# The step at which a 32x32 transpose reads its columns, and the engine that rounds w_out

## The chip, the cores and the metric

The kernel runs on one core of a Trainium2 chip. The metric is the time of the program on the device in microseconds (us): the median of several runs, lower is better. A core has five engines that work side by side, each in the fixed order in which its instructions were placed: TensorE (PE: matmuls, with weight loads, PEld), VectorE (DVE), ScalarE (ACT), GpSimd (POOL) and SyncE (SP, which issues DMAs). They wait for one another by semaphores.

## The reference, cut to what matters

```python
def _attn_ref(q, k, v, omega):            # 2 batches, 8 heads, 576 tokens, 64 channels, 128 features
    q_p, k_p = phi(q * scale), phi(k * scale)       # phi: exp of a projection, less its maximum
    kv = einsum('bhsm,bhsd->bhmd', k_p, v)
    z = sum(k_p, axis=2)
    return einsum('bhsm,bhmd->bhsd', q_p, kv) / (einsum('bhsm,bhm->bhs', q_p, z)[..., None] + 1e-06)

def _moe_ref(x, w1, w2, w3, w_out):       # x: 1152 x 512; w3: 1024 x 1024; w_out: 1024 x 512
    h = (x @ w1) * (x @ w2) @ w3
    return h @ w_out

def _moe2_ref(x, domain_probs, w1, w2):   # 4 experts, weighted by normalised domain_probs
    return sum(p[:, e:e+1] * (maximum(x @ w1[e], 0) @ w2[e]) for e in range(4))
```

The result of the attention goes through `_moe_ref`, and that through `_moe2_ref`. The weights w1, w2, w3 and w_out arrive as 64-bit floats.

## The kernel before, in words

Large products are made in three passes: each operand is split into a high part, rounded to the type fp32r, and a low part, the rest, in the same type; high by low, low by high and high by high are added up in PSUM. `split(hi, lo, src)` makes the parts: line 81 copies `src` to `hi` on ScalarE, with rounding, and line 82 subtracts `hi` from `src` on VectorE, or on the engine that is given (`eng`).

`from_f64` loads a 128 x 512 piece of 64-bit numbers as pairs of 32-bit words (tile `f`, of tag `f64`, three buffers) and builds 32-bit floats from them: line 100 scales the high words on ScalarE, line 101 shifts the low words on VectorE (`f64e`), and line 102 joins the two on VectorE. Within a partition, neighbouring high words lie 8 bytes apart. `load_w64` calls `from_f64` and `split`; `load_wo` does so for eight pieces of w_out (`wof`, then `wo`), `load_w12` for w1 and w2 (`w12f`, `w`), both with the subtraction on GpSimd.

`fold(m)` multiplies w3 by w_out ahead of time, in eight blocks (matmuls of line 211). It needs w3 transposed; `fold_transposed(u)` makes the 16 pieces. It loads a piece (`w3f`), and line 194 transposes it on VectorE in 32x32 squares (`w3t`). The columns of one square must be every fourth column of the piece. The kernel before reorders while it builds the floats: through `by_group`, lines 100 and 101 read the words at a step of 32 bytes and write them side by side, so that line 194 reads step by step:

```python
by_group = lambda x: x.rearrange("p (j c g) -> p j g c", j=4, g=4)
r = from_f64([rows[:, :, f:f + P] for f in first], "w3f", by_group)
nc.vector.transpose(t, r)
```

After that `split` makes the parts of `w3T` (line 81 on ScalarE, line 82 on VectorE), which are the weights of line 211.

The program has three stages. In the first (some 0 to 160 us) eight head pairs go through the attention: transposes and products on TensorE, maxima on VectorE (line 301, `mx`), exponentials on ScalarE (line 307, `ek` and `eq`), normalisation on VectorE (lines 378 to 380, `xs`), then transposition (`ps_x`) and a split into `xt`. `place_v` copies v on GpSimd (line 413, `va`). The table `BESIDE` says which loads (`o` for w_out, `w` for w1 and w2), folds (`f`) and gated products (`b`) are placed beside which pair. A scheduler of the framework then sets each engine's order from its own estimate of the instructions' times, so that a change to one instruction can move others on all engines. The second stage is the rest of the gated products, the third the four experts; they do not use `from_f64`, but for the last of w1 and w2.

Of the kernel before, what the change touches and what calls it, by code (L numbers as in the profile page):

```python
# [8 lines left out]
F32 = mybir.dt.float32  # L9
# [3 lines left out]
ACTF = mybir.ActivationFunctionType  # L13
ALU = mybir.AluOpType
AX = mybir.AxisListType

HI, LO = 0, 1
# [28 lines left out]
def attention_moe_kernel(ctx: ExitStack, tc: tile.TileContext, q, k, v, omega, mw1, mw2, mw3, mwo, probs, ew1, ew2, out):  # L46
    nc = tc.nc
# [5 lines left out]
    P = 128  # L53
# [22 lines left out]
    def bank(tag):  # L76
        return ps_p.tile([P, 512], F32, tag=tag, name="ps_" + tag, bufs=BANKS[tag])

    def split(hi, lo, src, eng=None):

        nc.scalar.activation(out=hi, in_=src, func=ACTF.Copy)  # L81
        (eng or nc.vector).tensor_tensor(out=lo, in0=src, in1=hi.bitcast(F32), op=ALU.subtract)  # L82

    def order_like(t, src):
        return t if len(src.shape) == 2 else t.rearrange("p (j g c) -> p j g c", j=src.shape[1], g=src.shape[2])

    def from_f64(srcs, name, order=lambda x: x):


        r = cv.tile([P, 512, 2], U32, tag="f64", name="f64", bufs=3)  # L90
        rows = P // len(srcs)
        for i, src in enumerate(srcs):
            o = r[i * rows:(i + 1) * rows].rearrange("p (k c) w -> p k (c w)", k=src.shape[1])
            nc.sync.dma_start(out=o, in_=src.bitcast(U32))
        low, high = order(r[:, :, 0]), order(r[:, :, 1])
        f = cv.tile([P, 512], F32, tag="f64f", name=name, bufs=2)
        e = cv.tile([P, 512], U32, tag="f64e", name="f64e", bufs=2)
        fb = f.bitcast(U32)

        nc.scalar.activation(out=order_like(f, high), in_=high.bitcast(F32), func=ACTF.Prelu, scale=2.0**-112, alpha=2.0**32)  # L100
        nc.vector.tensor_scalar(out=order_like(e, low), in0=low, scalar1=29, scalar2=None, op0=ALU.logical_shift_right)  # L101
        nc.vector.scalar_tensor_tensor(out=fb, in0=fb, scalar=3, in1=e, op0=ALU.logical_shift_left, op1=ALU.bitwise_or)
        return f

    def load_w64(pool, srcs, name, eng):
        f = from_f64(srcs, name + "f")
        t = pool.tile([P, 2, 512], F32R, tag=pool.name, name=name)
        split(t[:, HI], t[:, LO], f, eng=eng)
        return t


# [26 lines left out]
    w1_p = mctx.enter_context(tc.tile_pool(name="w1", bufs=8, side="right"))  # L138
# [3 lines left out]
    w12, hid, wo, w3o, x2, xf = {}, {}, [], [], {}, {}  # L142

    def load_w12(g):

        for w, src in enumerate((mw1, mw2)):
            src = src[:, g * P:(g + 1) * P].rearrange("(k p) c -> p k c", p=P)
            t = load_w64(w1_p, [src], "w12", nc.gpsimd)
            w12[w, g] = t.rearrange("p a (k c) -> p a k c", k=KD)

    def load_wo():


        hf, g = divmod(len(wo), 4)
        rows = mwo[hf * 512:(hf + 1) * 512].rearrange("(p g) d -> g p d", g=4)[g]
        wo.append(load_w64(w1_p, [rows.unsqueeze(1)], "wo", nc.gpsimd))

    def gated(a_p, bufs, b, g, tags):

        pool = xt_p if len(hid) < XT_BUFS - 2 * KD else h_p  # L160
        ht = hid[b, g] = pool.tile([P, 2, S], F32R, tag=pool.name, name="hid")
        halves = []
        for w in range(2):
            bs = [bank(tags[2 * w + c]) for c in range(2)]
            for kk in range(KD):
                for n, (x, y) in enumerate(PASSES):
                    for c in range(2):
                        nc.tensor.matmul(  # L168
                            out=bs[c][:, :HS], lhsT=w12[w, g][:, x, kk], rhs=xt[b][kk][:, y, c * HS:(c + 1) * HS],
                            start=(kk == 0 and n == 0), stop=(kk == KD - 1 and n == 2),  # L170
                        )
            for c in range(2):
                if w == 0:
                    t = a_p.tile([P, HS], F32, tag="a", name="a", bufs=bufs)
                    nc.scalar.activation(out=t, in_=bs[c][:, :HS], func=ACTF.Copy)
                    halves.append(t)
                else:
                    t, s = halves[c], slice(c * HS, (c + 1) * HS)
                    nc.vector.tensor_tensor(out=t, in0=bs[c][:, :HS], in1=t, op=ALU.mult)  # L179
                    split(ht[:, HI, s], ht[:, LO, s], t)  # L180
# [3 lines left out]
    def fold_transposed(u):  # L184

        m, hf = divmod(u, KF // 4)
        rows = mw3[m * P:(m + 1) * P].rearrange("(j r) f -> r j f", r=SQ)
        first = [hf * 512 + i * P for i in range(4)]  # L190
        by_group = lambda x: x.rearrange("p (j c g) -> p j g c", j=4, g=4)
        r = from_f64([rows[:, :, f:f + P] for f in first], "w3f", by_group)
        t = cv.tile([P, 512], U32, tag="f64e", name="w3t", bufs=2).bitcast(F32)
        nc.vector.transpose(t, r)
        t = t.rearrange("p (j g r) -> p g j r", j=4, g=4)
        wt = cv.tile([P, 2, 512], F32R, tag="w3T", name="w3T", bufs=2)
        hi, lo = (wt[:, x].rearrange("p (g j r) -> p g j r", j=4, g=4) for x in (HI, LO))
        split(hi, lo, t)
        w3T.append(wt)

    def fold(m):

        po = bank(("po", "w")[m % 2])
        n = 0
        for hf in range(KF // 4):
            u = m * (KF // 4) + hf
            while len(w3T) < min(u + 2, KF * (KF // 4)):
                fold_transposed(len(w3T))
            for g in range(4):
                for a, c in PASSES:  # L210
                    nc.tensor.matmul(  # L211
                        out=po, lhsT=w3T[u][:, a, g * P:(g + 1) * P], rhs=wo[hf * 4 + g][:, c],
                        start=(n == 0), stop=(n == 3 * KF - 1),
                    )
                    n += 1
        t = w3_p.tile([P, 2, 512], F32R, tag="w3o", name="w3o", bufs=KF)
        split(t[:, HI], t[:, LO], po)
        w3o.append(t)
# [51 lines left out]
    with ExitStack() as actx:  # L270
# [93 lines left out]
        for b in range(B):  # L364
            t = st.tile([P, H, D1], F32, name=f"vt{b}")
# [164 lines left out]
        for n in range(len(pairs) + 1):  # L530
# [32 lines left out]
            with ExitStack() as order:  # L563

                for ins in (*u.mark, loaded) if u else ():
                    order.enter_context(tc.issue_after(ins))
                for s in BESIDE.get(n, "").split():
                    if s[0] == "w":
                        load_w12(int(s[1]))
                    elif s[0] == "o":  # L570
                        load_wo()
                    elif s[0] == "f":
                        fold(int(s[1]))
                    else:
                        gated(at, 2, int(s[1]), int(s[2]), ("w", "po") * 2)
# [319 lines left out]
```

## Time and profile before

| | |
|---|---|
| median of 3 runs | 669.84 us (669.25 to 671.47) |
| profiled execution: its own time | 670.11 us |
| its span (first to last instruction) | 668.3 us |
| mean granted TensorE clock | 0.996 |
| busy, share of the span | PE 98%, weight loads 94%, DVE 69%, ACT 63%, POOL 18% |

The span is the profiled execution without what lies around it (1.8 us). Busy shares are means over all stages; a busy PE in the profile is one with a matmul in flight, whose end is modelled. A row of a timeline gives the start of a few like instructions, how long they took together, engine, line, tiles, and in brackets how long the engine had been idle just before and what ended that.

### The profile page before, as it was taken

The page shows a single profiled execution, that of the slowest core. Times are in us where ns is not written, and L with a number is a line of the kernel's source. Part 1 is how long each engine was busy: PE and PEld are TensorE (multiplying, and loading weights), DVE is VectorE, ACT ScalarE, POOL GpSimd, SP SyncE. Part 2 cuts the span into 40 slices and gives each one's busy share as a digit, 9 for nine tenths or more (in the row PEclk, how much of TensorE's full clock was granted, in tenths as well). Part 3 has the DMA queues.
Part 4 walks back from the last instruction along what each step waited for, and adds up shares of the span by engine and source line. Part 5 has one row for each costly group of instructions (what it writes and reads, how often), then busy time and mean ns, then how long its engine had stood idle before and what let it go on. Part 6 is the DMA issues. An engine that isn't in the chain of part 4 may idle for free.

```text
span 668.3 us, 12377 instructions
## 1 busy us (share of the span) xinstructions
PE 655.3 (98%) x4831; PEld 628.2 (94%) x4831; DVE 463.4 (69%) x770; ACT 422.0 (63%) x895; POOL 122.8 (18%) x145
## 2 busy tenths in 40 slices
PE   8999999999999999999999999999999999999997
PEld 6788888899999999999899999999999998999997
DVE  3869867776562134357959868868689588687695
ACT  5899648683552234247768768778587777686740
POOL 2321000131240000000022231331331312314200
PEclk9998999999999999999999999999999999999999
DMA  9868433445110002003154484682883855737725
GB/s 253 268 180 206 122 94 95 127 135 182 59 38 1 1 1 64 1 1 94 64 141 129 65 137 99 113 150 40 157 143 32 152 117 90 138 75 105 126 54 174
DMA packets 58090, 70.59 MB, mean 106 GB/s; under 512 B 8816, under 2 KB 43120, under 8 KB 58032
## 3 DMA queue, kind: packets, MB, share of 16 engines
q1 hardware_dynamic: 44704, 49.05, 25.0%
q0 software_dynamic: 12640, 20.19, 20.6%
q8 instruction: 38, 0.62, 0.4%
q10 hardware_dynamic: 688, 0.56, 0.3%
q14 instruction: 20, 0.16, 0.1%
HBM read 47.24 MB, written 22.54 MB: 104 GB/s over the span
## 4 chain that ended last, share of the span: by engine, by line
PE 82%; DVE 4%; issue 4%; ACT 4%; DMA 3%; POOL 1%; SPq 1%; DVEq 0%; ACTq 0%; POOLq 0%
PE ps_f L807 6%; PE ps_f L725 6%; PE ps_po L211 3%; PE ps_x L725 3%; PE ps_w L725 3%; PE ps_et L725 3%; PE ps_et L807 3%; PE ps_t L807 3%; PE ps_kv L807 3%; PE ps_x L807 3%; PE ps_kv L725 3%; PE ps_t L725 3%; PE ps_po L725 3%; PE ps_w L807 3%; PE ps_w L211 3%
## 5 line engine op out<-in xcount | busy, mean ns | idle before, releaser
L759 POOL DMA_DIRECT2D out_dram<-o x98 | 81.6, 901 | 355.5 <-DVE o L784 173.3
L82 DVE TENSOR_TENSOR hs<-hd,hs 128x1024 fp32r<-128x1024 f32 x48 | 58.3, 1218 | 1.6 <-ACT hs L81 1.6
L81 ACT ACTIVATE hs<-hd 128x1024 fp32r<-128x1024 f32 x48 | 50.6, 1056 | 5.7 <-DVE hd L621 4.6
L709 ACT ACTIVATE hd<-hd 128x288 f32<-128x288 f32 x96 | 40.7, 438 | 9.0 <-DVE hd L707 8.7
L725 PE MATMUL ps_f<-x,w1e 128*128 128x288 f32 x288 | 46.2, 294 | 0.0
L621 DVE TENSOR_TENSOR hd<-hd 128x512 f32<-128x512 f32 x64 | 43.9, 686 | 0.8
L621 DVE TENSOR_TENSOR raw<-raw 128x512 f32<-128x512 f32 x64 | 43.9, 686 | 0.5
L807 PE MATMUL ps_f<-w2e,hs 128*128 128x256 f32 x288 | 43.2, 282 | 0.0
L82 DVE TENSOR_TENSOR w2e<-raw,w2e 128x1024 fp32r<-128x1024 f32 x32 | 38.8, 1218 | 5.4 <-ACT w2e L81 5.3
L725 PEld LDWEIGHTS ps_f<-x,w1e 128*128 128x128 f32 x288 | 40.9, 188 | 0.1
L807 PEld LDWEIGHTS ps_f<-w2e,hs 128*128 128x128 f32 x288 | 38.5, 191 | 0.1
L81 ACT ACTIVATE w2e<-raw 128x1024 fp32r<-128x1024 f32 x32 | 33.1, 1054 | 6.3 <-DVE raw L621 3.2
L168 PE MATMUL ps_po<-xt,w 128*128 128x288 f32 x144 | 35.1, 296 | 0.0
L168 PE MATMUL ps_w<-xt,w 128*128 128x288 f32 x144 | 34.9, 297 | 0.0
L82 POOL TENSOR_TENSOR w<-w12f,w 128x512 fp32r<-128x512 f32 x16 | 22.3, 1404 | 65.4 <-ACT w L81 65.4
L82 DVE TENSOR_TENSOR w1e<-raw,w1e 128x1024 fp32r<-128x1024 f32 x24 | 29.3, 1220 | 5.8 <-ACT w1e L81 5.8
L81 ACT ACTIVATE hid<-a 128x288 fp32r<-128x288 f32 x32 | 13.0, 441 | 29.4 <-DVE a L179 29.2
L101 DVE TENSOR_SCALAR f64e<-f 128x512 uint32<-128x512 uint32 x40 | 24.4, 617 | 9.9 <-DMA f<-in_moe_w_dram 7.2
L81 ACT ACTIVATE w1e<-raw 128x1024 fp32r<-128x1024 f32 x24 | 25.4, 1057 | 6.2 <-issue 2.6
L168 PEld LDWEIGHTS ps_po<-xt,w 128*128 128x128 f32 x144 | 25.6, 189 | 0.1
L168 PEld LDWEIGHTS ps_w<-xt,w 128*128 128x128 f32 x144 | 25.3, 188 | 0.0
L781 ACT ACTIVATE o<-ps_f,pr 128x256 f32<-128x256 f32 (+1 forms) x37 | 17.8, 481 | 11.6 <-PE ps_f L807 7.4
(275 smaller groups left out, 1803.6 us busy)
## 6 DMA issues: line engine op xcount, KB each, us to landing
raw<-in_moe_w_dram SPq DMA_DIRECT2D x32, 512.0 KB, 5.4
out_dram<-o POOLq DMA_DIRECT2D x56, 256.0 KB, 5.1
f<-in_moe_w_dram SPq DMA_DIRECT2D x64, 128.0 KB, 3.3
f<-in_moe_w_dram SPq DMA_DIRECT2D x16, 512.0 KB, 4.6
out_dram<-o POOLq DMA_DIRECT2D x42, 128.0 KB, 4.5
f<-in_moe_w_out_dram SPq DMA_DIRECT2D x8, 512.0 KB, 6.5
kr<-in_k_dram SPq DMA_DIRECT2D x8, 256.0 KB, 5.0
vr<-in_v_dram SPq DMA_DIRECT2D x8, 256.0 KB, 5.1
```

The costliest lines, as they stand in the source:

```text
L81: nc.scalar.activation(out=hi, in_=src, func=ACTF.Copy)
L82: (eng or nc.vector).tensor_tensor(out=lo, in0=src, in1=hi.bitcast(F32), op=ALU.subtract)
L101: nc.vector.tensor_scalar(out=order_like(e, low), in0=low, scalar1=29, scalar2=None, op0=ALU.logical_shift_right)
L168: nc.tensor.matmul(out=bs[c][:, :HS], lhsT=w12[w, g][:, x, kk], rhs=xt[b][kk][:, y, c * HS:(c + 1) * HS], start=(kk == 0 and n == 0), stop ...
L211: nc.tensor.matmul(out=po, lhsT=w3T[u][:, a, g * P:(g + 1) * P], rhs=wo[hf * 4 + g][:, c], start=(n == 0), stop=(n == 3 * KF - 1),)
L621: nc.vector.tensor_tensor(out=o, in0=x, in1=y, op=op)
L709: nc.scalar.activation(out=h, in_=src, func=ACTF.Relu)
L725: nc.tensor.matmul(out=ps, lhsT=w1t[a][:, x, kk, g * P:(g + 1) * P], rhs=x2[b, kk][:, y, s], start=(k in "125" and kk == 0 and n == 0), st ...
L759: dma = nc.gpsimd.dma_start(out=out[toks, d], in_=src[rows], **({} if fresh else dict(accum_op=ALU.add))).ins
L781: nc.scalar.activation(out=o, in_=ps, func=ACTF.Copy, scale=pr[:, t, e:e + 1])
L807: nc.tensor.matmul(out=ps, lhsT=t[a][:, x, g, j * P:(j + 1) * P], rhs=w2t[b][:, y, g], start=(k in "15" and g == 0 and n == 0), stop=(k in ...
```

## The change

`from_f64` loses its reordering: all pieces, those of w3 too, are now built in the order in which they are loaded, at a step of 8 bytes. The reordering moves to the input of the transpose, which now reads its columns at a step of four 32-bit numbers, 16 bytes. Apart from that, `split` can round the high part on another engine, and `load_wo` asks for GpSimd: both instructions of that split are now on GpSimd.

```diff
-    def split(hi, lo, src, eng=None):
+    def split(hi, lo, src, eng=None, high=None):
-        nc.scalar.activation(out=hi, in_=src, func=ACTF.Copy)
+        if high is None:
+            nc.scalar.activation(out=hi, in_=src, func=ACTF.Copy)
+        else:
+            high.tensor_copy(out=hi, in_=src)
         (eng or nc.vector).tensor_tensor(out=lo, in0=src, in1=hi.bitcast(F32), op=ALU.subtract)
...
-        low, high = order(r[:, :, 0]), order(r[:, :, 1])
+        low, high = r[:, :, 0], r[:, :, 1]
...
-        nc.scalar.activation(out=order_like(f, high), in_=high.bitcast(F32), func=ACTF.Prelu, scale=2.0**-112, alpha=2.0**32)
-        nc.vector.tensor_scalar(out=order_like(e, low), in0=low, scalar1=29, scalar2=None, op0=ALU.logical_shift_right)
+        nc.scalar.activation(out=f, in_=high.bitcast(F32), func=ACTF.Prelu, scale=2.0**-112, alpha=2.0**32)
+        nc.vector.tensor_scalar(out=e, in0=low, scalar1=29, scalar2=None, op0=ALU.logical_shift_right)
...
-        wo.append(load_w64(w1_p, [rows.unsqueeze(1)], "wo", nc.gpsimd))
+        wo.append(load_w64(w1_p, [rows.unsqueeze(1)], "wo", nc.gpsimd, nc.gpsimd))
...
-        by_group = lambda x: x.rearrange("p (j c g) -> p j g c", j=4, g=4)
-        r = from_f64([rows[:, :, f:f + P] for f in first], "w3f", by_group)
+        r = from_f64([rows[:, :, f:f + P] for f in first], "w3f")
...
-        nc.vector.transpose(t, r)
+        nc.vector.transpose(t, r.rearrange("p (j c g) -> p j g c", j=4, g=4))
```

The scheduler's order moves with it. Line numbers of the attention are one lower in the kernel after (line 307 becomes 306), and lines 81 and 82 become 82 and 85, with the new copy on 84.

The first place is ScalarE between the tail's exponentials and those of the third head pair (`kva`, `ek`, `eq`), where the first three pieces of w_out are made. Before:

```order
L447 ACTIVATE kva<-ps_kv 128x130
L81 ACTIVATE wo<-wof 128x512
L307 ACTIVATE ek<-ps_f,mx 128x128 x4
L81 ACTIVATE wo<-wof 128x512
L307 ACTIVATE ek<-ps_f,mx 128x128 x4
L100 ACTIVATE wof<-f_267 128x512
L81 ACTIVATE wo<-wof 128x512
L307 ACTIVATE eq<-ps_f,mx 128x128 x4
```

The same place after:

```order
L446 ACTIVATE kva<-ps_kv 128x130
L306 ACTIVATE ek<-ps_f,mx 128x128 x8
L100 ACTIVATE wof<-f_267 128x512
L306 ACTIVATE eq<-ps_f,mx 128x128 x4
L446 ACTIVATE kva<-ps_kv 128x130
```

The three copies `wo` have left ScalarE. On GpSimd they stand as copies of line 84; the first two stand ahead of the first two subtractions.

The second place is ScalarE where w3 begins, beside the fourth head pair. Before:

```order
L100 ACTIVATE wof<-f_584 128x512
L454 ACTIVATE eT<-ps_et 128x512
L81 ACTIVATE xt_76<-ps_x 128x512
L100 ACTIVATE w3f<-f_595 128x512
L307 ACTIVATE eq<-ps_f,mx 128x128 x4
L284 ACTIVATE qT<-ps_t 128x512
L81 ACTIVATE wo<-wof 128x512
L307 ACTIVATE eq<-ps_f,mx 128x128 x4
```

After:

```order
L453 ACTIVATE eT<-ps_et 128x512
L82 ACTIVATE xt_76<-ps_x 128x512
L306 ACTIVATE eq<-ps_f,mx 128x128 x4
L283 ACTIVATE qT<-ps_t 128x512
L100 ACTIVATE wof<-f_584 128x512
L306 ACTIVATE eq<-ps_f,mx 128x128 x4
L100 ACTIVATE w3f<-f_595 128x512
```

The last `wof` and the first `w3f` now stand behind the first `eq`.

The third place is VectorE at the same moment. Before:

```order
L101 TENSOR_SCALAR f64e<-f_595 128x512
L301 TENSOR_REDUCE mx<-ps_f 128x4
L102 SCALAR_TENSOR_TENSOR wof<-wof,f64e 128x512
L301 TENSOR_REDUCE mx<-ps_f 128x4
L82 TENSOR_TENSOR xt_76<-ps_x,xt_76 128x512
L102 SCALAR_TENSOR_TENSOR w3f<-w3f,f64e 128x512
L194 STREAM_TRANSPOSE w3t<-w3f 128x512
```

After:

```order
L101 TENSOR_SCALAR f64e<-f_595 128x512
L300 TENSOR_REDUCE mx<-ps_f 128x4
L85 TENSOR_TENSOR xt_76<-ps_x,xt_76 128x512
L300 TENSOR_REDUCE mx<-ps_f 128x4
L102 SCALAR_TENSOR_TENSOR wof<-wof,f64e 128x512
```

The split of `xt_76` now stands ahead of the second maximum and of line 102. From the first fold on (58.8 us of the trace before) the order on PE, DVE and ACT differs at many places: the matmuls of line 211 stand between other pieces of the attention than before.

## Rows read from the trace of the kernel before

**Rows 1.** Page: granted clock of TensorE in 40 slices of 16.7 us, in tenths.

```profile
PEclk9998999999999999999999999999999999999999
```

**Rows 2.** Windows: stretch, its length, busy time by engine, clock, DMA.

```profile
20.00:60.00 40.00, 37.06 (x240) 32.14 (x239) 31.87 (x63) 36.91 (x102) 12.53 (x11) 0.96 0.76 207
60.00:100.00 40.00, 40.00 (x222) 33.66 (x221) 32.52 (x67) 23.41 (x45) 0.62 (x1) 1.00 0.47 126
100.00:160.00 60.00, 59.02 (x451) 53.79 (x451) 44.49 (x89) 40.78 (x95) 11.89 (x9) 1.00 0.45 135
```

**Rows 3.** Timeline of TensorE, its waits between 20 and 60 us.

```profile
26.06 0.60 PE L116 MATMUL ps_x<-ident,xs 128*128 128x128 f32 x4
27.39 1.13 PE L295 MATMUL ps_f<-om,qT 128*128 128x256 f32 x4 [0.73 <-ACT eq L307]
...
29.56 1.13 PE L295 MATMUL ps_f<-om,qT 128*128 128x256 f32 x4 [0.60 <-ACT eq L307]
...
33.98 0.84 PE L116 MATMUL ps_et<-ident,eq 128*128 128x128 f32 x3 [0.59 <-ACT eq L307]
...
50.47 0.33 PE L116 MATMUL ps_et<-ident,eq 128*128 128x128 f32 x1 [0.66 <-ACT eq L307]
51.16 1.08 PE L461 MATMUL ps_x<-kva,eT 128*128 128x65 f32 x8 [0.36 <-DVE xt L82]
...
52.29 1.85 PE L295 MATMUL ps_f<-om,kT 128*128 128x256 f32 x4
```

**Rows 4.** Timeline of ScalarE ahead of those waits.

```profile
22.48 0.63 ACT L81 ACTIVATE wo<-wof 128x512 fp32r<-128x512 f32 x1 [0.52 <-DVE wof L102]
23.14 1.14 ACT L307 ACTIVATE ek<-ps_f,mx 128x128 f32<-128x128 f32 x4
...
26.20 1.14 ACT L307 ACTIVATE eq<-ps_f,mx 128x128 f32<-128x128 f32 x4
...
28.32 1.19 ACT L307 ACTIVATE eq<-ps_f,mx 128x128 f32<-128x128 f32 x4
...
32.99 0.68 ACT L513 ACTIVATE eTt<-ps_et 128x512 f32<-128x512 f32 x1
...
48.99 1.17 ACT L100 ACTIVATE w3f<-f 128x512 f32<-128x512 f32 x1
50.02 1.17 ACT L307 ACTIVATE eq<-ps_f,mx 128x128 f32<-128x128 f32 x4
```

**Rows 5.** Timeline of VectorE at the same places.

```profile
18.96 0.68 DVE L102 SCALAR_TENSOR_TENSOR wof<-wof,f64e 128x512 uint32<-128x512 uint32 x1
19.76 0.43 DVE L101 TENSOR_SCALAR f64e<-f 128x512 uint32<-128x512 uint32 x1
...
20.70 1.75 DVE L102 SCALAR_TENSOR_TENSOR wof<-wof,f64e 128x512 uint32<-128x512 uint32 x1
22.37 0.68 DVE L301 TENSOR_REDUCE mx<-ps_f 128x4 f32<-128x512 f32 x1
...
48.51 0.70 DVE L301 TENSOR_REDUCE mx<-ps_f 128x4 f32<-128x512 f32 x1
...
50.31 0.70 DVE L82 TENSOR_TENSOR xt<-ps_x,xt 128x512 fp32r<-128x512 f32 x1
```

**Rows 6.** Timeline of GpSimd beside the long line 102 of rows 5.

```profile
17.80 0.61 POOL L413 COPY va<-vr 128x512 f32<-128x512 f32 x1 [7.01 <-PE ps_kv L445]
20.63 1.27 POOL L82 TENSOR_TENSOR wo<-wof,wo 128x512 fp32r<-128x512 f32 x1 [2.22 <-ACT wo L81]
```

**Rows 7.** Groups of ScalarE: line 100 at steps of 32 and 8 bytes.

```profile
L100 ACT ACTIVATE w3f<-f 128x512 f32<-128x512 f32 x16 | 19.0, 1197 | 0.8 <-DVE d L379 0.6 <-ACT xt L81 0.2
L100 ACT ACTIVATE w12f<-f 128x512 f32<-128x512 f32 x16 | 10.8, 681 | 6.4 <-POOL w L82 6.4
```

**Rows 8.** Groups of VectorE between 48 and 127 us, the pieces of w3.

```profile
L194 DVE STREAM_TRANSPOSE w3t<-w3f 128x512 f32<-128x512 f32 x16 | 11.3, 706 | 0.2
L101 DVE TENSOR_SCALAR f64e<-f 128x512 uint32<-128x512 uint32 x17 | 10.8, 634 | 1.0 <-DMA f<-in_moe_w_dram 0.9
```

More of the change, by code (lines that the diff above doesn't have):

```diff
@@ L77, in bank, with from_f64 @@
         return ps_p.tile([P, 512], F32, tag=tag, name="ps_" + tag, bufs=BANKS[tag])
-    def split(hi, lo, src, eng=None):
-        nc.scalar.activation(out=hi, in_=src, func=ACTF.Copy)
+    def split(hi, lo, src, eng=None, high=None):
[3 more added lines that the diff above has]
+            high.tensor_copy(out=hi, in_=src)
         (eng or nc.vector).tensor_tensor(out=lo, in0=src, in1=hi.bitcast(F32), op=ALU.subtract)
-    def order_like(t, src):
-        return t if len(src.shape) == 2 else t.rearrange("p (j g c) -> p j g c", j=src.shape[1], g=src.shape[2])
-    def from_f64(srcs, name, order=lambda x: x):
+    def from_f64(srcs, name):
         r = cv.tile([P, 512, 2], U32, tag="f64", name="f64", bufs=3)
@@ L98, in from_f64, with load_w64 @@
         fb = f.bitcast(U32)
-        nc.scalar.activation(out=order_like(f, high), in_=high.bitcast(F32), func=ACTF.Prelu, scale=2.0**-112, alpha=2.0**32)
-        nc.vector.tensor_scalar(out=order_like(e, low), in0=low, scalar1=29, scalar2=None, op0=ALU.logical_shift_right)
+        nc.scalar.activation(out=f, in_=high.bitcast(F32), func=ACTF.Prelu, scale=2.0**-112, alpha=2.0**32)
+        nc.vector.tensor_scalar(out=e, in0=low, scalar1=29, scalar2=None, op0=ALU.logical_shift_right)
         nc.vector.scalar_tensor_tensor(out=fb, in0=fb, scalar=3, in1=e, op0=ALU.logical_shift_left, op1=ALU.bitwise_or)
         return f
-    def load_w64(pool, srcs, name, eng):
+    def load_w64(pool, srcs, name, eng, high=None):
         f = from_f64(srcs, name + "f")
         t = pool.tile([P, 2, 512], F32R, tag=pool.name, name=name)
-        split(t[:, HI], t[:, LO], f, eng=eng)
+        split(t[:, HI], t[:, LO], f, eng=eng, high=high)
         return t
```

## The prediction, made before the kernel ran

> **What bounds the kernel now.** I read the granted clock by slices first, then the busy time of windows, then the timelines of the engines where TensorE stood still. The clock is full but for a dip in the fourth slice and the edges [rows 1]. TensorE is what the time consists of: it is busy for all of 60 to 100 us and for 59.02 of the next 60 us, while VectorE has 22.99 us and ScalarE 35.81 us idle in those 100 us [rows 2]. So the folds, in which all 16 pieces of w3 are made, hide nearly all the work of the other two engines, and what the change saves there can at most win the 0.98 us that TensorE lacks. The stretch that matters is 20 to 60 us: TensorE is busy for 37.06 of 40 us there, and ScalarE, with 36.91, as much [rows 2]. The missing 2.94 us are five waits: 0.73, 0.60, 0.59, 0.66 and 0.36, four of them for `eq` on ScalarE and the last for the split of `xt` on VectorE [rows 3]. I call them A, B, C, D and E. The exponentials are late because pieces of w_out, and at the end of w3, stand among them. Nothing of the change touches the experts, and I carry their time over unchanged.
>
> **The change part by part.**
>
> *Eight copies leave ScalarE.* Each took 0.63 us there [rows 4], some 5 us in all, before 54 us. What that is worth has to be followed wait by wait, for a copy that stood in an idle moment gives nothing.
>
> Wait A. The exponential that ends it runs at 26.20 [rows 4] and follows a chain that slipped at 20.70: line 102 took 1.75 us instead of 0.68 [rows 5], beside GpSimd's first subtraction of 1.27 us [rows 6]. The maximum at 22.37 stood behind it, and so did the copy at 22.48 and `ek` at 23.14 [rows 4, 5]. After the change the first floats are ready at 19.64, the end of the first line 102 [rows 5], and GpSimd then copies, and may not subtract before it has copied the second piece too. If the copy takes what `va` takes, 0.61 us for as many numbers [rows 6], it is over at some 20.3, before line 102 begins at 20.70. That one then takes 0.68 and the maximum comes about 1.0 us earlier; no copy stands before `ek`, and VectorE takes the next maximum ahead of line 102 of the third piece. So `eq` comes about 1.0 us earlier, at 25.2, and TensorE, which has its transposes at 26.06 [rows 3], finds it under way. I take all of A. A wait's bracket begins at a modelled end: four transposes are counted as 0.60 us, and would be followed sooner, so I add 0.15 and take 0.9.
>
> Wait B. The `eq` at 28.32 stands behind the copy of `xt`, which needs those same transposes. They hardly move, so I take 0.2 us of 0.60. Wait C: `eq` at 33.48, behind `eTt` at 32.99 [rows 4], which itself waits for a transposition just finished on TensorE. Two copies disappear ahead of it, and nothing comes of it: I take 0.
>
> Waits D and E. Before `eq` at 50.02 stands the first `w3f` with 1.17 us [rows 4]; its maximum was done at 49.21 [rows 5]. After the change `w3f` stands behind it, and `eq` can begin at about 49.2, 0.8 us sooner. The split of `xt` at 50.31 [rows 5] stood behind one maximum and a line 102, and now comes right after the first maximum, at about 49.3, a whole 1.0 us sooner. Of 0.66 and 0.36, with the same 0.15 on each, 1.3 us in all, some 0.2 remain, since TensorE now makes three transposes there at once. I take 1.1.
>
> *Line 100 of w3 at 8 bytes.* 1197 ns become 681 [rows 7]: 16 times 0.52 is 8.3 us less on ScalarE. The one that counts is moved anyway (D). The others lie under TensorE's matmuls. In 100 to 160 us I take 0.2 of the 0.98 us.
>
> *Line 101 of w3 at 8 bytes.* 634 ns on average [rows 8] become 0.43 us, as for w_out [rows 5]: 16 times 0.2 is 3.3 us less on VectorE, hidden by the 22.99 us. Without that cover they would count whole.
>
> *The transpose at 16 bytes.* The trace shows none. Nearest below is itself at consecutive numbers, 706 ns [rows 8]. Nearest above is line 100, whose step of 32 bytes costs 0.52 us more than 8 [rows 7], so 1.2 us. Which row is nearer? Line 101 is on the same engine and reads at 32 bytes in 634 ns [rows 8], under the 706 ns in which the transpose now moves as many numbers. VectorE thus fetches a number from so far apart at the rate at which the transpose needs them. I take 0.71 and no cost, and keep 1.2 for a rival.
>
> [...]
>
> *The copy on GpSimd.* Between 0.61 us (`va`, no rounding) and 1.27 (the subtraction, which rounds but reads two inputs) [rows 6]; I take 0.61, since one input is read. At 1.27 the first copy ends at 20.9 and meets line 102 for 0.2 us, and A shrinks to about 0.5. GpSimd is busy 12.53 of 40 us [rows 2], so its five more us fit. The first fold starts some us after the last subtraction of w_out ends, so it waits for it in neither case.
>
> *Order.* From the first fold on all orders differ. The work is the same; whether new waits appear is the open term. Before, such an order lost 0.98 us between 60 and 160 us, and I take the same.
>
> Sum: 0.9 + 0.2 + 0 + 1.1 + 0.2 = 2.4 us. From the profiled 670.11 that gives 667.7. This execution lay 0.27 over the median, so in medians 669.84 - 2.4 = 667.4 us.
>
> **The rivals.**
>
> *The dip goes too.* [...] It begins right behind D and E, when TensorE had stood still. [...] For it: the order of the two. Against: A to C caused no dip.
>
> *New waits eat it.* The first `w3f` now stands behind two groups of exponentials and the last `wof`, so the first transposed piece comes 2 to 3 us later (twice 1.17 less what overlaps [rows 4], and a line 100), while TensorE is to reach the first fold earlier. If it stands still for 2 us in the folds that had no idle time before, 669.4, no change.
>
> *Slower: the transpose pays for its step.* If it takes 1.2 us, VectorE has 8.3 - 3.3 = 5.0 us more between 50 and 125 us. Its mean reserve hides that only if it lies where it is needed; each fold waits for its own piece, one transpose after the other. If all 5.0 reach TensorE the time is 667.4 + 5.0 = 672.4. It decides from about 0.9 us a transpose: 16 times 0.2 is then what line 101 gives back, and beyond it VectorE loses.
>
> **How the numbers follow.** Forecast 0.43, with a range of its own of 666.7 to 668.7 (below: most of the rest of B and C won too; above: A halved and 0.9 us of new waits). Dip gone 0.20; new waits 0.25, from 668.4 to 671; slower 0.12. A change of 0.3%, 2.0 us, is about the least that a measurement tells from none here: faster is below 667.8. That takes 0.31 of the forecast, all of the dip's 0.20 and a little of the rest: 0.53. Within it: 0.12 of the forecast and most of the new waits, 0.34. Slower 0.13, the transpose and a very bad order. The range of 665.4 to 670.8 leaves out a dip gone with more gains, and the slower cases.
>
> **What would show it.** Right: `w3f` at about 0.68 and line 101 at 0.43 us; `w3t` near 0.71; copies of line 84 near 0.61; line 102 beside them at 0.68 and not 1.75; TensorE's idle time in 20 to 60 us at 1.2 us or less, with only B and C left; idle time of 60 to 160 us about 1 us. Wrong: `w3t` over 0.9; idle time or waits for `w3T` inside the folds; waits D and E still there because the maximum or the transposes came later than I think; or the first fold standing still for its piece.

## The result: slower by half a per cent

Six runs of the kernel after have a median of 674.3 us (672.4 to 675.35), six of the kernel before beside them 671.26. The ratio is 1.0052, with a 95% interval of 1.0029 to 1.0074: slower, and outside the range of the prediction. (All ratios here are estimated from all runs taken side by side, and can differ by some 0.1% from the quotient of two medians, which is 1.0045 here.) The profiled execution of after took 673.34 us, with a span of 671.5 us, 3.2 us more than before.

I read the profile after in the order of the prediction. The granted clock by slices answers to [rows 1]:

```profile
PEclk9999999899999999999999999999999999999999
```

There is again one dip, but it stands in the eighth slice, not the fourth. By the mean clocks of the windows (0.96 over 40 us before, 0.97 over 60 us after) I estimate that it costs about as much as the old one, 4% of 40 us and 3% of 60 us, so these two profiles do not differ by it. The windows answer to [rows 2], the first 20 us added:

```profile
0.00:20.00 20.00, 16.45 (x94) 12.34 (x95) 8.46 (x17) 10.82 (x31) 4.87 (x18) 1.00 0.96 266
20.00:60.00 40.00, 38.05 (x262) 33.62 (x261) 31.21 (x62) 32.56 (x95) 17.44 (x19) 1.00 0.70 201
60.00:100.00 40.00, 39.43 (x221) 32.22 (x221) 35.40 (x71) 21.73 (x55) 0.62 (x1) 1.00 0.54 136
100.00:160.00 60.00, 56.45 (x409) 50.57 (x408) 41.35 (x81) 35.73 (x86) 11.35 (x9) 0.97 0.39 115
```

From 20 to 60 us TensorE lacks 1.95 us instead of 2.94: the gain is there. From 60 to 160 us it lacks 0.57 + 3.55 = 4.12 us instead of 0.98: this loss is three times the gain. (In the first 20 us it lacks 3.55 us where before lacked 2.53. This stretch varies among profiles whatever the order: 16.66 to 17.47 us busy in five kernels with the copy on ScalarE, 16.45 to 18.71 in three with the order of after. Of the 3.2 us between these two profiles 1.0 lies here; but kernel one below, which loses as much, is busier here than before, with 18.71 us, so I do not count it to the change.)

TensorE's timeline between 28 and 51 us answers to [rows 3]:

```profile
29.44 1.13 PE L294 MATMUL ps_f<-om,qT 128*128 128x256 f32 x4 [0.53 <-ACT eq L306]
31.23 0.33 PE L116 MATMUL ps_et<-ident,eq 128*128 128x128 f32 x1 [0.66 <-ACT eq L306]
...
34.19 0.85 PE L116 MATMUL ps_et<-ident,eq 128*128 128x128 f32 x3 [0.51 <-ACT eq L306]
...
47.67 0.66 PE L116 MATMUL ps_t<-ident,qr 128*128 128x128 f32 x4 [0.26 <-DVE kT L281]
...
50.16 0.84 PE L116 MATMUL ps_et<-ident,eq 128*128 128x128 f32 x3
50.84 1.00 PE L460 MATMUL ps_x<-kva,eT 128*128 128x65 f32 x8
```

Waits A, D and E are gone, as predicted. B and C are still there, and two have come, 0.66 us behind B and 0.26 for `kT`. At the other end of the first stage TensorE's timeline shows what was not foreseen:

```profile
121.73 1.17 PE L210 MATMUL ps_w<-wo,w3T 128*128 128x512 f32 x4
...
123.88 1.16 PE L318 MATMUL ps_f<-omh,kT 64*128 64x128 f32 x16 [0.19 <-ACT eq L331]
125.97 0.66 PE L116 MATMUL ps_et<-ident,eq 128*128 128x128 f32 x4 [0.93 <-ACT eT L453]
127.19 1.11 PE L460 MATMUL ps_x<-kva,eT 128*128 128x65 f32 x8 [0.57 <-DVE xt L85]
129.59 4.62 PE L210 MATMUL ps_w<-wo,w3T 128*128 128x512 f32 x12 [1.29 <-DVE w3T L85]
```

Four waits in 6 us, 2.98 us together, and then a fold whose twelve matmuls take 4.62 us at a mean clock of 0.63, where twelve at a clock of 1.00 took 3.04 (at 80.72 us of the same trace): the dip. The chain of work through this place, each row the start, the length, the engine, the tile and the line:

```profile
121.65 0.62 ACT eq L331 x2
...
122.41 1.41 ACT eq L331 x5
123.83 0.56 ACT w3f L100
...
124.41 0.70 DVE w3f L102
...
125.14 1.09 DVE w3t L193
126.23 0.31 DVE f64e L101
126.54 0.60 DVE xt L85
127.14 1.20 DVE mx L329 x2
...
128.85 0.69 DVE w3T L85
...
129.59 4.62 PE ps_w L210 x12
```

This is the last piece of w3, made and split for the last fold: line 100 behind eight exponentials, the transpose with 1.09 us, then the split, which stands behind `xt` and two maxima on VectorE. Line 100 of that piece is not later than before, where it also began at 123.7 us, and the transpose even began earlier, at 125.14 against 125.73 us. But the split comes 1.0 us later, at 128.85 instead of 127.87 us. VectorE's split of this piece before:

```profile
127.87 0.68 DVE L82 TENSOR_TENSOR w3T<-w3t,w3T 128x512 fp32r<-128x512 f32 x1
```

What TensorE had to do meanwhile differs too. Its timeline before, at the same time:

```profile
124.48 1.00 PE L445 MATMUL ps_kv<-va,ek 128*128 128x65 f32 x8
...
126.75 1.16 PE L319 MATMUL ps_f<-omh,kT 64*128 64x128 f32 x16
127.84 0.66 PE L116 MATMUL ps_et<-ident,eq 128*128 128x128 f32 x4
128.34 0.60 PE L116 MATMUL ps_x<-ident,xs 128*128 128x128 f32 x4
128.69 2.56 PE L211 MATMUL ps_w<-wo,w3T 128*128 128x512 f32 x10
```

Before, TensorE came to its attention work ahead of this fold at 124.48 us and went through 4 us of it without a wait: the sums of line 445 stood first, and their inputs were there. After, it comes to it at 122.74 us. Some 4 us of attention work stand there too, but most of it waits for fresh results of ScalarE and VectorE, and the sums of line 444 follow behind the fold (at 135.63 us).

The durations, as groups by line of the whole execution, and line 101 between 48 and 127 us (answering to [rows 7] and [rows 8]):

```profile
L193 DVE STREAM_TRANSPOSE w3t<-w3f 128x512 f32<-128x512 f32 x16 | 17.6, 1099 | 0.2
L100 ACT ACTIVATE w3f<-f 128x512 f32<-128x512 f32 x16 | 10.9, 689 | 8.7 <-DVE w3t L193 5.8 <-DVE d L377 2.3 <-DMA f<-in_moe_w_dram 0.6
L84 POOL CAST wo<-wof 128x512 fp32r<-128x512 f32 x8 | 5.4, 687 | 15.4 <-DVE wof L102 11.5 <-DVE d L377 3.9
L102 DVE SCALAR_TENSOR_TENSOR wof<-wof,f64e 128x512 uint32<-128x512 uint32 x8 | 5.4, 683 | 1.1 <-ACT wof L100 1.1
L101 DVE TENSOR_SCALAR f64e<-f 128x512 uint32<-128x512 uint32 x17 | 7.2, 422 | 1.0 <-DMA f<-in_moe_w_dram 1.0
```

The transpose takes 1099 ns and not 0.71 us. The others came about as predicted (the copy with 0.69 us for 0.61). So two suspects are left, the order and the transpose, with line 100's gain against them.

### The profile page after: what moved, and what is told of

Same layout as the page of the kernel before. It is cut to its first block, busy times and chain, and to the rows that moved or that the text cites. A ratio compares the mean times of both kernels' runs of the same rounds, so it can differ in the third digit from the quotient of the medians.

```text
span 671.5 us, 12381 instructions
## 1 busy us (share of the span) xinstructions
PE 655.5 (98%) x4831; PEld 627.6 (93%) x4831; DVE 463.3 (69%) x770; ACT 410.3 (61%) x887; POOL 127.4 (19%) x153
## 4 chain that ended last, share of the span: by engine, by line
PE 85%; DVE 6%; ACT 3%; DMA 3%; issue 2%; SPq 1%; POOL 0%; DVEq 0%; ACTq 0%
PE ps_f L806 6%; PE ps_f L724 6%; PE ps_x L724 3%; PE ps_w L724 3%; PE ps_et L724 3%; PE ps_et L806 3%; PE ps_kv L806 3%; PE ps_t L806 3%; PE ps_x L806 3%; PE ps_w L168 3%; PE ps_kv L724 3%; PE ps_f L168 3%; PE ps_po L168 3%; PE ps_t L724 3%; PE ps_po L724 3%; PE ps_w L806 3%
## 5 line engine op out<-in xcount | busy, mean ns | idle before, releaser
L210 PE MATMUL ps_w<-wo,w3T 128*128 128x512 f32 x96 | 26.0, 421 | 1.3 <-DVE w3T L85 1.3
L101 DVE TENSOR_SCALAR f64e<-f 128x512 uint32<-128x512 uint32 x40 | 22.2, 563 | 6.6 <-DMA f<-in_moe_w_dram 3.4
```

What stands on the lines that cost most here:

```text
L101: nc.vector.tensor_scalar(out=e, in0=low, scalar1=29, scalar2=None, op0=ALU.logical_shift_right)
L210: nc.tensor.matmul(out=po, lhsT=w3T[u][:, a, g * P:(g + 1) * P], rhs=wo[hf * 4 + g][:, c], start=(n == 0), stop=(n == 3 * KF - 1),)
```

## The experiments

My theory: the order that the scheduler made once the copy had left ScalarE costs more than the copy gives; the transpose adds a little, and line 100 at 8 bytes gives some of it back. The rival: the transpose's 16 × 0.39 = 6.3 us is the loss, and the waits of the new order are its consequence.

The built orders allow a clean separation. Before, after, and the first four kernels below have only two orders of instructions between them: with the copy on ScalarE that of before, with the copy on GpSimd that of after. How lines 100, 101 and 194 step through a piece moves no instruction.

**One: the copy alone.** The kernel before with the diff of `split`, `load_w64` and `load_wo` and nothing else.

```diff
-        wo.append(load_w64(w1_p, [rows.unsqueeze(1)], "wo", nc.gpsimd))
+        wo.append(load_w64(w1_p, [rows.unsqueeze(1)], "wo", nc.gpsimd, nc.gpsimd))
```

> The kernel before with the second part of the change alone: the high parts of w_out are rounded by GpSimd, w3 is built and transposed as before. Theory P (the price of the transpose's step made the change slow, and the part for w_out is what I took it for): the transpose stays at 706 ns, TensorE's idle time in 20 to 60 us falls from 2.94 to some 2 us, and the ratio to the kernel before is 0.996 to 0.999. Theory O (the order that the scheduler makes of it, with GpSimd's copies in VectorE's way, made it slow): 1.003 or more, with new waits after 60 us.

Measured: 674.43 us, ratio 1.0065 (1.0043 to 1.0087). Its window from 100 us, and two rows of TensorE's timeline in it:

```profile
100.00:160.00 60.00, 57.42 (x408) 51.53 (x406) 39.01 (x80) 37.93 (x86) 11.58 (x9) 0.94 0.38 115
```

```profile
126.51 1.11 PE L119 MATMUL ps_et<-ident,eq 128*128 128x128 f32 x4 [1.39 <-ACT eT L457]
...
129.76 4.69 PE L214 MATMUL ps_w<-wo,w3T 128*128 128x512 f32 x12 [0.43 <-DVE w3T L85]
```

The loss is all there with the transpose untouched, and TensorE waits at the same place, ahead of the same fold. In this profile the idle time is smaller than in after (2.58 us against 3.55), and the dip behind it is longer (clock 0.94 over the 60 us). `eT` is later than in after, because line 100 of `w3f` stands ahead of it with 1.2 us. The rival falls as the whole cause.

**Two: the steps alone.** The kernel after with the copy back on ScalarE.

```diff
-        wo.append(load_w64(w1_p, [rows.unsqueeze(1)], "wo", nc.gpsimd, nc.gpsimd))
+        wo.append(load_w64(w1_p, [rows.unsqueeze(1)], "wo", nc.gpsimd))
```

> The change without its second part: w3 is read at 8 bytes and transposed at 16, the high parts of w_out stay on ScalarE. P: the transpose takes about 1.1 us as in the kernel after, and the ratio to the kernel before is 1.005 to 1.010, at least that of the whole change. O, with GpSimd to blame: 0.998 to 1.002.

Measured: 669.93 us, ratio 0.9985 (0.9964 to 1.0005), with transposes of 1096 ns. The windows from 60 to 160 us:

```profile
60.00:100.00 40.00, 40.00 (x222) 33.69 (x222) 34.74 (x69) 20.50 (x48) 0.79 (x2) 1.00 0.47 126
100.00:160.00 60.00, 59.63 (x453) 54.57 (x452) 45.15 (x88) 38.19 (x94) 12.04 (x10) 1.00 0.43 131
```

TensorE lacks 0.37 us here, less than before (0.98), though each transpose takes 0.39 us more.

**Three and four: the steps taken apart.** The third is after with the transpose reading number by number (line 100 still at 8 bytes), the fourth is before with the transpose at 16 bytes (line 100 still at 32). The third leaves the regrouping of w3's columns out and the fourth does it twice, so columns of w3 meet other rows of w_out; the work is the same in kind and amount.

```diff
-        nc.vector.transpose(t, r.rearrange("p (j c g) -> p j g c", j=4, g=4))
+        nc.vector.transpose(t, r)
```

```diff
-        nc.vector.transpose(t, r)
+        nc.vector.transpose(t, r.rearrange("p (j c g) -> p j g c", j=4, g=4))
```

> The kernel after, but the transpose reads its squares from neighbouring numbers, so that the columns of w3 are paired with the wrong rows of w_out: its time is read, not its numbers. Every engine has the same instructions in the same order as in the kernel after; only the step of 16 transposes differs. P: the transpose is back at about 0.71 us, the waits of TensorE at 80 us and from 123 to 134 us are gone or below 1.5 us in all, and the ratio to the kernel before is 0.992 to 0.997. O: the waits stay, 1.003 to 1.006.

> The kernel before, but its transpose reads at a step of 16 bytes what was already reordered, so that the columns of w3 are paired with the wrong rows of w_out: its time is read, not its numbers. Every engine has the same instructions in the same order as in the kernel before. P: the transpose takes about 1.1 us, VectorE has 6.3 us more in the folds, TensorE waits for w3T there, and the ratio to the kernel before is 1.004 to 1.010. O: the step is hidden, 0.999 to 1.002.

Measured: the third 672.21 us, ratio 1.0025 (1.0006 to 1.0044); the fourth 672.44 us, ratio 1.0026 (1.0005 to 1.0046), its transposes 1093 ns. Both miss the ranges of both theories and lie nearer to O: the step is not all hidden, but it is not the loss. The six kernels together, with the mean time of those runs whose mean granted clock was 0.997, and the number of runs in which it was 0.999 or 1.000:

| copy and order | line 100 of w3 | transpose reads | kernel | ratio | at clock 0.997 (runs) | at 0.999 or 1.000 |
|---|---|---|---|---|---|---|
| ScalarE, of before | 32 bytes | side by side | before | 1 | 670.68 us (13) | 9 of 34 |
| ScalarE, of before | 32 bytes | 16 bytes | four | 1.0026 | 672.56 us (8) | 4 of 12 |
| ScalarE, of before | 8 bytes | 16 bytes | two | 0.9985 | 670.54 us (3) | 6 of 12 |
| GpSimd, of after | 32 bytes | side by side | one | 1.0065 | 674.30 us (6) | 0 of 11 |
| GpSimd, of after | 8 bytes | side by side | three | 1.0025 | 672.53 us (5) | 4 of 12 |
| GpSimd, of after | 8 bytes | 16 bytes | after | 1.0052 | 673.88 us (5) | 0 of 6 |

(The runs of before counted here are the 34 beside one to four; after was run at another time.)

Each edit is priced twice, by differences of the ratios. The transpose: +0.26% (four less before) and +0.27% (after less three), 1.8 us. Line 100 at 8 bytes: -0.41% (two less four) and -0.40% (three less one), 2.7 us. The copy with its order: +0.65% (one less before) and +0.67% (after less two), 4.4 us. The sum, 0.26 - 0.41 + 0.65 = +0.50%, meets the measured +0.52%, but that is the same comparison once more, since the three edits lead from before to after. One difference by itself is uncertain by some 0.2 to 0.3%, as the intervals show; that the pairs agree makes it firmer. That they agree to 0.02% is luck: by quotients of medians the pairs are +0.33 and +0.16, -0.37 and -0.33, +0.63 and +0.50%. I price line 101's step with line 100's, since the same edit moved both.

One rival remains: that the kernels differ by the dip of the clock alone. The last two columns settle most of it. One and after have no run at 0.999 or 1.000, so part of their loss is the clock. But at the same clock of 0.997, as far as three to 13 runs tell, the copy with its order still costs 3.6 us (one less before) and 3.3 (after less two), the transpose 1.9 and 1.4, and line 100 still gives 2.0 and 1.8.

The third kernel's window, and its fold in TensorE's timeline:

```profile
100.00:160.00 60.00, 56.83 (x422) 51.21 (x421) 40.52 (x83) 36.62 (x88) 11.39 (x9) 1.00 0.41 121
```

```profile
129.82 3.06 PE L210 MATMUL ps_w<-wo,w3T 128*128 128x512 f32 x12 [1.29 <-DVE w3T L85]
```

It has no dip (clock 1.00) although TensorE lacks 3.17 us, and the same fold waits 1.29 us for `w3T` as in after; so the dip is not the loss, but comes on top of it in some runs.

**Five: another order from about 122 us on.** If the cause is the order at the last fold, another order there must take the loss back. The table of the work beside each pair now puts the load of the first parts of w1 and w2 (`w0`) ahead of the last fold, and the scheduler places the rest anew:

```diff
-BESIDE = {..., 5: 'f5 f6', 6: 'f7 w0', 7: 'w1 b00 w2', 8: 'b01 w3'}
+BESIDE = {..., 5: 'f5 f6', 6: 'w0 f7', 7: 'w1 b00 w2', 8: 'b01 w3'}
```

> The kernel after with one entry of the table swapped: beside the seventh pair the first load of w1 and w2 stands before the last fold, not behind it. GpSimd's copies, all steps, and the order up to about 115 us stay. Theory W (the waits of TensorE from 123 to 134 us, for eT, for xt and for the last w3T, are the price of the new order): these waits fall from 3.6 us to below 1.5, the clock does not fall behind them, and the ratio to the kernel before is 0.997 to 1.001. Rival G (GpSimd's copies cost by what they hold up before 60 us, or the whole order is worse): 1.004 to 1.006, as in the kernel after.

Measured: 671.25 us, ratio 1.0006 (0.9988 to 1.0025). The order on the engines that compute differs from after's only from about 122 us on. Its window, and TensorE's timeline:

```profile
100.00:160.00 60.00, 58.66 (x427) 53.41 (x425) 41.06 (x83) 35.22 (x84) 11.38 (x9) 0.97 0.42 128
```

```profile
125.24 0.66 PE L116 MATMUL ps_et<-ident,eq 128*128 128x128 f32 x4 [0.93 <-ACT eT L453]
...
127.10 3.11 PE L168 MATMUL ps_po<-xt,w 128*128 128x288 f32 x12
...
132.88 3.00 PE L210 MATMUL ps_w<-wo,w3T 128*128 128x512 f32 x12
```

Matmuls of a gated product (line 168, which uses w1 and w2) now fill the time in which the last piece is made, the fold no longer waits for it, and 0.46% of the loss comes back with the copy still on GpSimd and the transposes still at 16 bytes. That the dip would go too was expected and did not happen in this profile: it now slows line 168 (3.11 us for twelve that take 1.75 in after). Whether the same swap would win as much in the order of before was not run; but TensorE lacks only 0.98 us there from 100 to 160 us, at full clock [rows 2], so there is less to win.

**Six: another priority.** The attention of a pair has a priority of its own, set by `offset`: -100 for the first six pairs and 400 from the seventh on. Here 400 begins with the sixth.

```diff
-            with tc.high_priority(offset=-100 if n < 6 else 400):
+            with tc.high_priority(offset=-100 if n < 5 else 400):
```

> The kernel after with the attention's raised priority from the sixth pair on instead of the seventh; GpSimd's copies and all steps stay, and the order differs from about 80 us on. W: another order without last pieces of w3 among the attention's copies on ScalarE; TensorE's idle time of 60 to 160 us is about 1 to 2 us instead of 4.1, and the ratio to the kernel before 0.998 to 1.002. G: 1.004 to 1.006.

Measured: 669.81 us, ratio 0.9988 (0.9971 to 1.0006). The order differs from after's from about 48 us on VectorE and 68 us on TensorE, and not from 80 us as I expected. Its profile (671.53 us, above its own median) still lacks 3.26 us from 100 to 160 us, at other places; the idle time that I expected was wrong, the ratio was not. A second order thus takes back what the first lost, but its profile does not show where. Part of it is the clock: seven of its 12 runs have a mean clock of 0.999 or 1.000, none of after's six, and the profiled one has 0.997.

**Seven to ten: no step at all.** If w_out's rows are loaded in another order, w3 needs no regrouping: line 100 at 8 bytes and the transpose number by number, and each column of w3 still meets its row of w_out. The seventh loads each piece in one transfer with one more dimension in its source, the eighth is that with the GpSimd copy and the table of experiment five; the ninth uses four transfers a piece, the tenth is that with the GpSimd copy and the priority of experiment six. Of the two source forms the lines that choose the rows are shown.

```diff
-        rows = mwo[hf * 512:(hf + 1) * 512].rearrange("(p g) d -> g p d", g=4)[g]
+        rows = mwo[hf * 512:(hf + 1) * 512].rearrange("(i g c) d -> g i c d", i=4, g=4)[g]
...
-        nc.vector.transpose(t, r.rearrange("p (j c g) -> p j g c", j=4, g=4))
+        nc.vector.transpose(t, r)
```

```diff
-        rows = mwo[hf * 512:(hf + 1) * 512].rearrange("(p g) d -> g p d", g=4)[g]
+        at = [hf * 512 + i * P + g * SQ for i in range(4)]
+        rows = [mwo[a:a + SQ].unsqueeze(1) for a in at]
...
-        nc.vector.transpose(t, r.rearrange("p (j c g) -> p j g c", j=4, g=4))
+        nc.vector.transpose(t, r)
```

> No reordering anywhere: the rows of w_out are loaded so that the columns of a 32x32 square of w3 may be neighbours; line 100 and line 101 read w3 at 8 bytes, the transpose reads number by number, and the high parts of w_out stay on ScalarE. The order on every compute engine is that of the kernel before. Theory S (in a fixed order the steps add up: 16-byte transposes cost 0.26% and line 100 at 8 bytes wins 0.4%, as the four runs so far give): 0.9985 - 0.0027 = 0.996 to the kernel before. Rival H (the gains are of the order of what the runs scatter, and hidden where TensorE has other work): 0.998 to 1.000.

> The run before this one without reordering, the rows of w_out loaded to fit, so that the transpose reads number by number: the same instructions in the same order on every compute engine. W and S together: 0.27% below the run before this one, 0.994 to 0.998 to the kernel before. G: 1.001 to 1.003.

> As the run with no reordering and the high parts on ScalarE, but each piece of w_out comes in four loads of 32 partitions, as those of w3 do, instead of one load with a split outer dimension. The order on every compute engine is that of the kernel before. S: the late loads of w_out are gone, the transpose takes 0.71 us, line 100 of w3 0.68, and the ratio to the kernel before is 0.995 to 0.998. H: 0.998 to 1.000. If small loads are what was slow there, and not the split dimension: above 1.02 again.

> The run with the attention's priority raised from the sixth pair on, without reordering: four loads for a piece of w_out, and the transpose reads number by number; on every compute engine the order of that run. W and S together: 0.27% below that run's 0.9988, that is 0.994 to 0.998 to the kernel before. G or H: 0.998 to 1.001.

Measured: 696.48 us (1.0382, 1.0354 to 1.0410), 697.35 (1.0391, 1.0358 to 1.0424), 674.49 (1.0061, 1.0037 to 1.0086) and 673.89 (1.0069, 1.0042 to 1.0095). All are slower, and in all of them TensorE lacks more from 20 to 60 us than before, while loads are late. Of the seventh, the loads of v by queue, kind, count, size and median us from issue to landing, and its window:

```profile
vr<-in_v_dram SPq DMA_DIRECT2D x8, 256.0 KB, 14.9
```

```profile
20.00:60.00 40.00, 28.19 (x141) 24.09 (x142) 16.40 (x32) 22.71 (x64) 7.52 (x7) 0.74 0.44 144
```

With the one transfer a piece, v, which comes through the same queue, takes 14.9 us (16.5 in the eighth), 5.2 in after, and TensorE lacks 11.8 us there. How long the transfer itself takes, and why v is late behind it, the trace does not show. With four transfers v lands after 4.2 us, but a piece of w_out comes late. The ninth's window and its first wait:

```profile
20.00:60.00 40.00, 36.21 (x205) 30.88 (x204) 25.36 (x56) 31.62 (x89) 11.33 (x10) 0.85 0.78 202
100.00:160.00 60.00, 59.75 (x451) 54.57 (x451) 42.03 (x89) 39.71 (x102) 12.12 (x10) 1.00 0.39 115
```

```profile
24.06 1.89 PE L445 MATMUL ps_kv<-va,ek 128*128 128x65 f32 x8 [1.52 <-ACT ek L307]
```

The folds are as good as they can be, 0.25 us lacking from 100 to 160 us, and the early pairs pay for it: VectorE waits 1.96 us for a piece of w_out at 22.49 us, `ek` is late, and TensorE is slow behind its own wait: four matmuls of line 295 take 2.02 us at 26.17 and at 30.01 us, and 1.13 at 19.68, ahead of it (clock 0.85 from 20 to 60 us; this run, 676.15 us, lies above the median). The tenth lacks 4.30 us from 20 to 60 us, at a clock of 0.96, and 2.86 from 100 to 160 us.

**Eleven and twelve: where the transpose's price begins.** The kernel before with the transpose at 8 and at 32 bytes; again columns of w3 meet other rows of w_out.

```diff
-        nc.vector.transpose(t, r)
+        nc.vector.transpose(t, r.rearrange("p (j c g) -> p j g c", j=8, g=2))
```

```diff
-        nc.vector.transpose(t, r)
+        nc.vector.transpose(t, r.rearrange("p (j c g) -> p j g c", j=2, g=8))
```

> The kernel before with the transpose reading at a step of 8 bytes what was already reordered (the columns of w3 are paired with the wrong rows of w_out; its time is read). [...] Rival M (the price rises with the step): about 0.84 us, a third of the way to 16 bytes.

> The same with a step of 32 bytes. [...] M: 1.5 us or more.

One run each, 670.95 and 673.84 us. The tile `w3t` of both, with minimum, median and maximum in ns:

```profile
L194 DVE STREAM_TRANSPOSE w3t<-w3f x16: 678/708/725, 53.2 to 125.8; 128x512 f32<-128x512 f32 x16
```

```profile
L194 DVE STREAM_TRANSPOSE w3t<-w3f x16: 1093/1164/1224, 54.1 to 129.4; 128x512 f32<-128x512 f32 x16
```

At 8 bytes the transpose costs what it costs side by side (708 and 706 ns), at 16 it costs 1.10 us, at 32 hardly more (1.16). M, with 0.84 us at 8 bytes and 1.5 or more at 32, misses both. Of the steps tried, 16 bytes is the first that has a price.

## Why the prediction was wrong

**The step that failed: Order, "and I take the same".** I carried over the 0.98 us that the order of before lost from 60 to 160 us. The order after loses 4.12, and by the table the copy with its order costs 0.65%, 4.4 us, whichever way the steps go. Five shows that it is the order and not the copy by itself: rearranged from about 122 us on, when the last copy of w_out has been over for more than 60 us, the loss is 0.06% instead of 0.52%. The order costs in two ways: TensorE waits, and the clock is lower in the runs of one and after (0.995 to 0.997), which makes up some 1 us of the 4.4. The rival of new waits had the mechanism, but at the wrong place: I looked for them at the first fold, which does not stand still, and they came at the last. My range left 1 us above the time before for it, and 0.52%, 3.5 us, came: 0.98 us was the outcome of one order, not a property of the work.

**The transpose: "I take 0.71 and no cost."** It takes 1.10 us. The argument carried a rate from line 101 to another operation: line 101 is one that goes at 0.42 us when it reads at 8 bytes, and its 634 ns at 32 were already slowed; the transpose at 16 is slowed too. Its own runs give 708 ns at 8 bytes, 1.10 us at 16 and 1.16 at 32; why the price begins between 8 and 16, no run shows. The rival, which put line 100's 0.52 us on the transpose and so had 1.2 us, had the price nearly right and its effect too large: of 6.3 us on VectorE 1.8 reached the time, not all of it.

**Line 100: only the size was off.** It costs 0.69 us as predicted, but I let the rest be "hidden" and counted 0.2 us, besides its move in D. It gave 2.7 us, together with line 101. The chain above shows one place where it counts, between the exponentials and line 102 of the last piece. Busy shares had said that ScalarE has time to spare; but it has it elsewhere than where a piece is waited for.

**The waits of the first 60 us: right in kind.** A, D and E are gone, B and C stayed; the lack fell by 0.99 us where 2.2 were foreseen (0.9, 0.2 and 1.1), because 0.66 and 0.26 us came anew. In one, where line 100 stayed as it was, it fell by 0.14 us only. The copy takes 0.61 or 0.62 us six times out of eight, and 0.69 on average. The long line 102 of wait A is gone too. GpSimd's timeline and VectorE's after:

```profile
20.66 0.62 POOL L84 CAST wo<-wof 128x512 fp32r<-128x512 f32 x1 [1.72 <-DVE wof L102]
```

```profile
20.68 0.87 DVE L101 TENSOR_SCALAR f64e<-f 128x512 uint32<-128x512 uint32 x1
...
22.07 0.68 DVE L102 SCALAR_TENSOR_TENSOR wof<-wof,f64e 128x512 uint32<-128x512 uint32 x1
```

Line 102 takes 0.68 us. Instead line 101, beside the copy, takes 0.87 and not 0.43 [rows 5]. Why, the trace does not show; no wait of TensorE follows it here.

**The dip** did not vanish with D and E, it moved to 130 us in the profile (a clock of 0.63 from 129.59 to 134.21 us, where before has 0.52 from 52.29 to 54.14). No run shows the dip go with D and E, the rival with the chance of 0.20; the nearest is that the nine runs of before at 0.999 or 1.000 take 669.42 us on average and the 13 at 0.997 take 670.68, 1.3 us more. Why it comes is open: it differs among runs of one kernel (9 of 34 runs of before have a mean clock of 0.999 or 1.000, the others 0.994 to 0.997), and it follows waits in after, one and five, while three has waits of 0.93 and 1.29 us at the same two places and no dip.

Open also: where the 2.7 us of line 100 lie in full (between four and two TensorE's lack from 60 to 160 us falls from 1.58 to 0.37 us, which is 1.2 of them), and where six wins what it wins. The change as a whole has no version here that beats the kernel before for certain; two and six come nearest, and both their intervals hold 1.

## What to carry to other kernels

When an instruction changes its engine under a scheduler, price the new order by itself: what the old one lost says nothing of it, and it can lose more, 70 us further on, than the edit gives. Where runs differ in the granted clock, compare them at the same clock too. Kernels that share an order and differ in one step separate the price of a step from that of the order; two by two, each price is measured twice. Take the price of a strided read from the same operation on the same engine, or keep both ends open.

## What the runs showed of the hardware, unexpected

A transpose in 32x32 squares of 128x512 numbers reads at 8 bytes' step for nothing (706 and 708 ns), at 16 bytes for 0.39 us more, at 32 for 0.46. ScalarE's line 100, at 8 and 32 bytes, goes from 0.69 to 1.2 us. With one transfer a piece of w_out to 128 partitions, its source in two outer dimensions (4 by 32 rows), the loads of v took 14.9 and 16.5 us (seven and eight) instead of 5.2; with four transfers of 32 rows they took 4.2 and 5.0 (nine and ten). In the first 20 us TensorE's busy time varied by 2.3 us (16.45 and 18.71) between after and kernel one, which have the same order.
